# Batch 0's block attention in one pass per pair of heads, or in two passes over all heads

## The chip, the cores and the metric

One core of one Trainium2 chip runs the whole program. The metric is the device time in microseconds (us) of one execution, as the median of several runs. Engines: PE (TensorE), DVE (VectorE), ACT (ScalarE), POOL (GpSimd) and SP (SyncE, which here issues every load and store).

## What is computed

```python
# q, k, v: (4, 8, 576, 64); blocks of 64 tokens, block-causal
scores = np.where(mask, scale * q @ k.T, -1e9)      # mask: block_i >= block_j
attn = exp(scores - max) / (sum + 1e-9);  x = attn @ v      # x: (4*576, 512)
x = (sigmoid(x @ w_gate) * (x @ w_val)) @ w_out             # 512 -> 1536 -> 512
x = leaky_relu(x @ w_in) @ w_out2                           # 512 -> 2048 -> 512
```

All in float32. The weights must keep nearly float32 precision, so each weight unit and each activation is split into a high and a low float32r part, and a product is made of three matmuls.

## The kernel before, in words

The program is a list of operations, each with an engine (or a choice of two), a cost, a due time and the tiles that it uses. `Plan.order` (L127) then puts them in a row: again and again it takes the operation that can start first by its costs, and among those that can start at that moment the one with the smallest due time. That row is what each engine executes, strictly in its order. A tile comes from a `Ring` (L44) of a fixed number of buffers, and the tiles of a ring are given out in the order in which the program asked for them:

```python
if t.index != new[t.ring] or (k >= 0 and t.ring.tiles[k].left):   # L141
    waiting.add(o)
    return
```

so an operation that needs tile n of a ring waits until tile n-1 has been taken by its own first operation. The PSUM banks are rings too: `sc` (2 banks), `pa` (1), `tp` (2) and `mm` (3, L246).

`attention(b, ...)` (L332) works on a batch's eight heads in four pairs. `pair(i)` (L416) loads q and k of two heads (`tqk`, a ring of 3 buffers) and v (`tv`, a ring of 2) and handles the 576 queries in tiles: `query_tiles([0, 1])` (queries 0 to 255, keys up to 128 or 256), `query_tiles([2])`, `query_tiles([3])`, and `last_queries` (the last 64 queries of both heads together, all 576 keys). Each tile goes the same way:

- `scores`, L351: PE, q by k, into `sc` (batch 0 also uses `pa` for every third).
- `softmax`: DVE adds the mask and takes the row's extreme (L374); ACT makes the exponentials and their sum (L389); DVE adds 1e-9 and inverts (L399, L402); ACT or POOL multiplies (L407, L409).
- `transposed`, L500 (L458 for the last queries): PE transposes into `tp`; DVE or ACT copies out (`copy`, L296 for ACT, L298 for DVE).
- L522 (L472 for the last queries): PE, probabilities by v. In batch 0, the attention that stands alone, these go into `mm` banks.
- `split`: DVE or ACT writes the high part of x, DVE the low part (L309).

Batch 0's attention comes first (due times from 5 to 45 us); the attention of batches 1 to 3 is mixed into the matmuls of the batch before. The MLP's matmuls are `half_unit` (L917): one unit is 128 output columns, in two halves, tokens 0 to 255 and 256 to 575, each 12 matmuls into one `mm` bank (L938). The first gate units run all their first halves before the second ones (`by_half`). Each weight unit is loaded raw (`raw`, a ring of 3) and converted by ACT (`mag` L627, `rnd` L624), DVE (L628, L631, L635, split L298 and L309) and POOL (L641), then stored to `wd` for the later batches. All four engines thus share their time between attention and conversion.

Of the kernel before, what the change touches and what calls it, by code (L numbers as in the profile page):

```python
# [18 lines left out]
P = 128  # L19
BLK = 64  # L20
NKT = 5
# [177 lines left out]
def block_attention_then_two_mlps(  # L199
# [14 lines left out]
    B, H, _, D, S = qk.shape  # L214
# [69 lines left out]
    def load(t, dst, src, size, due, reads=(), writes=(), queue="sp"):  # L284
        if queue == "sp":
            op("sp", max(0.6, size / 320e3), lambda: nc.sync.dma_start(out=dst(), in_=src), reads, writes, [t], due, 1.8)
        else:
            op("act", 0.6, lambda: nc.scalar.dma_start(out=dst(), in_=src), reads, writes, [t], due, 1.8 + size / 320e3)
# [43 lines left out]
    def attention(b, start, length, alone):  # L332

        weight = [0.7, 0.9, 1.0, 1.1, 0.8]
        total = H // 2 * sum(weight)
        banks = [0]

        def bank():  # L340
            banks[0] += 1
            return (b_pa if alone and banks[0] % 3 == 0 else b_sc).tile()

        def scores(products, tqk, t):

            def f():
                for ps, col, row, a, q0, nq, k0, nk in products:
                    half = slice(a * D, a * D + D)  # L350
                    nc.tensor.matmul(  # L351
                        ps[row:row + nq, col:col + nk], lhsT=tqk[half, 0, q0:q0 + nq], rhs=tqk[half, 1, k0:k0 + nk],
                        start=True, stop=True,
                    )

            cost = 0.1 + sum(0.1 + 0.82e-3 * x[7] for x in products)
            used = list(dict.fromkeys(x[0] for x in products))
            op("pe", cost, f, [(tqk, 0), (tqk, 1)], used, [tqk, *used], t, kind="h")
# [54 lines left out]
                op(("act", "pool"), (0.24 + n / 1200, 0.25 + n / 1200), f, [r], [p_tok], [r, both], t + 2.6, port=("pool",))  # L413
            return [x[:2] for x in done]

        def pair(i):  # L416
            t_p = start + 2 * length * i / H

            t_end = 0.0 if alone else t_p + 2 * length / H
            at = [t_p + 2 * length * sum(weight[:c]) / (H * sum(weight)) for c in range(NKT)]  # L420

            tqk, tv = r_qk.tile(), r_v.tile()
            for a in range(2):
                load(
                    tqk, lambda a=a: tqk[a * D:a * D + D], qk[b, 2 * i + a].rearrange("s d n -> d s n"),
                    D * 2 * S * 4, t_p - 9, (), [(tqk, a)],
                )
            for a in range(2):
                load(tv, lambda a=a: tv[:, a], v[b, 2 * i + a], P * NKT * D * 4, t_p - 6, (), [(tv, a)])
            pas = {}  # L430

            def split(n0, n1, parts, t, p, reads):
# [47 lines left out]
            def query_tiles(cs):  # L480
                t = at[cs[0]]
                ps = [bank(), bank()]
                cols = dict(zip(cs, (0, P)))
                scores([(ps[a], cols[c], 0, a, c * P, P, 0, (c + 1) * P) for c in cs for a in range(2)], tqk, t)
                done = softmax([[(ps[a], cols[c], (c + 1) * P)] for c in cs for a in range(2)], True, t)
                for c in cs:
                    transposed(c, done[2 * cs.index(c):][:2], at[c])
# [41 lines left out]
                op("pe", cost, f, [(tv, 0), (tv, 1), *toks], [(pa, c)], [pa, tv, both], max(t + 5.2, t_end), kind="h")  # L529
                split(c0 * P, (c + 1) * P, ("C" if c0 else "A") if alone else "AC", max(t + 5.2, t_end) + 0.8, pa, [(pa, c)])  # L530

            for cs in ([0, 1], [2], [3]):
                query_tiles(cs)
            last_queries(at[NKT - 1])

        for i in range(H // 2):
            pair(i)

# [459 lines left out]


    attention(0, 5.0, FIRST, True)
    held, sl = {}, []
    sums_x = None
# [18 lines left out]
    for n, (u, half) in enumerate(order):  # L1023
        if n in stages:
            b = stages.index(n)
            length = starts[b + 1] - starts[b]
            if b:
                sg.append(r_sg.tile())
            if b < 2:
                sl.append(r_sg.tile(F32R))  # L1030
            if b == 0:
                attention(1, starts[0] + 3, length - SPREAD, False)
            elif b == 1:
                attention(2, starts[1] + 3, length / 2 - 3, False)
                attention(3, starts[1] + length / 2, length / 2 - SPREAD, False)
# [78 lines left out]
```

## Time and profile before

| what | value |
|---|---|
| median of 3 runs | 1036.53 us (1035.37 to 1037.73) |
| the profiled execution's own time | 1035.02 us |
| its span, first to last instruction | 1033.2 us |
| PE busy | 1015.0 us (98%) |
| DVE, ACT, POOL busy | 714.7, 529.0, 170.6 us |
| moved by DMA | 200.03 MB |

Busy times are those of the span. An engine's instructions overlap by a little, so the time that one takes of its engine is the distance from its start to the next start, which is a little less than its own duration. The profile's times are from the start of the span; the 1.8 us between span and own time lie around it.

### The profile page before, as it was taken

What the parts mean: (1) busy time and instruction counts of PE and PEld (TensorE: products, weight loads), DVE (VectorE), ACT (ScalarE), POOL (GpSimd) and SP (SyncE); (2) the same over time, 40 slices, a digit from 0 to 9 for tenths busy, and PEclk for the clock granted to TensorE, in tenths of its full rate; (3) what the DMA queues carried; (4) which work ended last, traced back from release to release, by engine and by line L of the source; (5) the groups of instructions that cost most, each with busy time, mean ns of one, the idle gap of its engine ahead of it and who ended that gap; (6) DMA issues with size and microseconds to landing.
All of it is one profiled execution on the core that took longest, in us unless ns stands there. A gap on an engine that the chain in (4) does not pass through costs nothing.

```text
span 1033.2 us, 20192 instructions
## 1 busy us (share of the span) xinstructions
PE 1015.0 (98%) x7680; PEld 939.7 (91%) x7680; DVE 714.7 (69%) x1767; ACT 529.0 (51%) x1187; POOL 170.6 (17%) x182
## 2 busy tenths in 40 slices
PE   7899999999999999999999999999999999999998
PEld 4579898999989889888988989999999999999998
DVE  6999899999987756467556448760844887163652
ACT  7987777687747564555556534242220454331320
POOL 3321122312231412112222102110200010000000
PEclk9999999999999999999999999999999999999999
DMA  8776878679787966566665445453441435251422
GB/s 246 239 242 232 313 267 272 214 245 312 257 286 273 307 226 225 193 187 216 227 207 186 144 143 188 144 187 98 154 164 62 154 108 188 72 164 65 164 79 93
DMA packets 69985, 200.03 MB, mean 194 GB/s; under 512 B 6912, under 2 KB 16128, under 8 KB 69888
## 3 DMA queue, kind: packets, MB, share of 16 engines
q1 hardware_dynamic: 69888, 198.73, 57.5%
q8 instruction: 61, 1.00, 0.4%
q14 instruction: 36, 0.29, 0.1%
HBM read 137.36 MB, written 61.34 MB: 192 GB/s over the span
## 4 chain that ended last, share of the span: by engine, by line
PE 83%; DVE 9%; ACT 4%; DMA 2%; issue 2%; POOL 0%; SPq 0%; ACTq 0%; DVEq 0%; POOLq 0%
PE mm L938 51%; PE mm L841 6%; PE tp L841 6%; PE sc L841 6%; PE sc L351 4%; PE pa L841 3%; PE tp L500 3%; PE pa L522 2%; DVE w L309 1%; DVE mag L635 1%; DVE both L374 1%; ACT both L389 1%; DVE mag L628 1%; ACT both L407 1%; PE tp L472 1%
## 5 line engine op out<-in xcount | busy, mean ns | idle before, releaser
L938 PE MATMUL mm<-x,w 128*128 128x256 f32 (+1 forms) x1920 | 271.1, 298 | 0.5 <-ACT gf L978 0.5
L938 PE MATMUL mm<-g,w 128*128 128x256 f32 (+1 forms) x1776 | 270.8, 298 | 0.0
L938 PEld LDWEIGHTS mm<-x,w 128*128 128x128 f32 x1920 | 257.0, 188 | 12.5 <-issue 4.9
L938 PEld LDWEIGHTS mm<-g,w 128*128 128x128 f32 x1776 | 245.7, 189 | 8.8 <-issue 2.0
L991 DVE TENSOR_TENSOR acc<-mm,acc 128x256 f32<-128x256 f32 (+1 forms) x160 | 72.6, 454 | 86.5 <-PE mm L938 85.8
L389 ACT ACTIVATE both<-both,nm 128x128 f32<-128x128 f32 (+2 forms) x144 | 83.0, 578 | 37.0 <-DVE nm L374 36.9
L641 POOL TENSOR_TENSOR wf<-mag,rnd 128x512 int32<-128x512 int32 x43 | 59.0, 1372 | 174.1 <-DVE mag L635 109.7
L841 PE MATMUL sc<-x,w 128*128 128x256 f32 (+1 forms) x480 | 76.3, 295 | 1.0 <-ACT v L296 1.0
L351 PE MATMUL sc<-qk 64*64 64x288 f32 (+4 forms) x356 | 69.3, 468 | 5.6 <-DMA qk<-in_qk 5.5
L309 DVE TENSOR_TENSOR g<-gf,g 128x576 fp32r<-128x576 f32 (+2 forms) x92 | 62.5, 685 | 17.3 <-ACT g L296 17.2
L374 DVE CUSTOM_DVE_ANT_0 both<-sc,mask 128x256 f32<-128x256 f32 (+3 forms) x133 | 59.1, 478 | 17.3 <-PE sc L351 17.3
L938 PE MATMUL mm<-sg,w 128*128 128x320 f32 (+1 forms) x416 | 70.2, 294 | 0.0
L841 PEld LDWEIGHTS sc<-x,w 128*128 128x128 f32 x480 | 67.8, 188 | 1.2 <-ACT v L296 1.2
L938 PE MATMUL mm<-qk,w 128*128 128x320 f32 (+1 forms) x384 | 66.8, 296 | 0.0
L296 ACT ACTIVATE g<-gf 128x576 fp32r<-128x576 f32 (+2 forms) x73 | 43.3, 596 | 45.2 <-DVE gf L965 23.0
L938 PEld LDWEIGHTS mm<-sg,w 128*128 128x128 f32 x416 | 60.5, 188 | 0.0
L409 POOL TENSOR_SCALAR both<-both,r 128x256 f32<-128x256 f32 (+4 forms) x54 | 36.8, 687 | 137.2 <-DVE r L402 101.0
L407 ACT ACTIVATE both<-both,r 128x512 f32<-128x512 f32 (+4 forms) x90 | 48.3, 575 | 17.3 <-DVE r L402 16.9
L938 PEld LDWEIGHTS mm<-qk,w 128*128 128x128 f32 x384 | 56.5, 189 | 0.0
L500 PE MATMUL tp<-ident,both 128*128 128x128 f32 x320 | 48.1, 280 | 5.0 <-ACT both L407 2.3
L627 ACT ACTIVATE mag<-raw 128x512 f32<-128x512 f32 x68 | 45.5, 669 | 12.3 <-DMA raw<-in_w 11.8
L309 DVE TENSOR_TENSOR w<-wf,w 128x512 fp32r<-128x512 f32 x68 | 49.0, 721 | 2.2 <-ACT w L296 1.9
(169 smaller groups left out, 1595.2 us busy)
## 6 DMA issues: line engine op xcount, KB each, us to landing
w<-wd SPq DMA_DIRECT2D x116, 512.0 KB, 4.2
raw<-in_w SPq DMA_DIRECT2D x68, 512.0 KB, 4.6
wd<-w SPq DMA_DIRECT2D x68, 512.0 KB, 4.2
ds<-raw SPq DMA_DIRECT2D x40, 512.0 KB, 4.8
w<-ds SPq DMA_DIRECT2D x40, 512.0 KB, 6.2
qk<-in_qk SPq DMA_DIRECT2D x32, 288.0 KB, 5.4
v<-in_v SPq DMA_DIRECT2D x32, 160.0 KB, 3.4
w<-wd SPq DMA_DIRECT2D x20, 256.0 KB, 3.6
```

What stands on the lines that cost most here:

```text
L296: nc.scalar.activation(dst(), src(), AF.Copy)
L309: engines[e].tensor_tensor(dst(), a(), f32(b()), ALU.subtract)
L351: nc.tensor.matmul(ps[row:row + nq, col:col + nk], lhsT=tqk[half, 0, q0:q0 + nq], rhs=tqk[half, 1, k0:k0 + nk], start=True, stop=True,)
L374: nc.vector.tensor_tensor_reduce(out=pt[:, n:n + width], in0=ps[:, col:col + width], in1=mask[:, 4 * P - width:] if masked else mask[:, :w ...
L389: nc.scalar.activation(pt[:, :n], pt[:, :n], AF.Exp, bias=nm[:, k - 1:k], scale=-1.0, accum_out=sm[:, i:i + 1],)
L407: nc.scalar.activation(pt[:, :n], pt[:, :n], AF.Copy, scale=r[:, i:i + 1])
L500: nc.tensor.transpose(tp[:, (j * m + k) * P:(j * m + k + 1) * P], tiles[a][0][:, j * P:(j + 1) * P], ident)
L627: op("act", c_act(n), lambda: nc.scalar.activation(mag[:], words(1).bitcast(F32), AF.Abs), [raw], [mag], [raw, mag], d - 8)
L641: engines[e].tensor_tensor(wf[:].bitcast(I32), mag[:].bitcast(I32), rnd[:], ALU.add)
L841: nc.tensor.matmul(p[:, :n], lhsT=wt[:, wl, col + k * P:col + (k + 1) * P], rhs=srcs[k][0]()[:, xl, hs], start=k == 0 and wl + xl == 0, st ...
L938: nc.tensor.matmul(ps[:, :n], lhsT=ws[:, wl, k * P:(k + 1) * P], rhs=srcs[k]()[:, xl, hs], start=k == 0 and wl + xl == 0, stop=k == 3 and ...
L991: op("dve", c_dve(n), lambda: nc.vector.tensor_tensor(a, ps[:, :n], a, ALU.add), [ps], toks_a, [ps], e)
```

## The change

`pair` takes a second argument, the query tiles that it handles. For batch 0 (`alone`) the four pairs are run through twice: first tiles 0 and 1 (queries 0 to 255) of all pairs, then tiles 2, 3 and the last queries. For the other batches there is still one pass. Each call of `pair` loads its own q, k and v: the first pass the first 256 tokens of them, the second all 576 tokens again. The due times are spread over the two passes in proportion to the tiles' weights.

```diff
-        def pair(i):
-            t_p = start + 2 * length * i / H
-
-            t_end = 0.0 if alone else t_p + 2 * length / H
-            at = [t_p + 2 * length * sum(weight[:c]) / (H * sum(weight)) for c in range(NKT)]
+        def pair(i, cs):
+            n, j = (S, NKT) if NKT - 2 in cs else ((cs[-1] + 1) * P, cs[-1] + 1)
+            share = sum(weight[cs[0]:j])
+            step = length * share / total
+            t_p = start + (length * (H // 2) * sum(weight[:cs[0]]) / total) + i * step
+
+            t_end = 0.0 if alone else t_p + step
+            at = [t_p + step * sum(weight[cs[0]:c]) / share for c in range(NKT)]
...
-                    tqk, lambda a=a: tqk[a * D:a * D + D], qk[b, 2 * i + a].rearrange("s d n -> d s n"),
-                    D * 2 * S * 4, t_p - 9, (), [(tqk, a)],
+                    tqk, lambda a=a: tqk[a * D:a * D + D, :, :n], qk[b, 2 * i + a].rearrange("s d n -> d s n")[:, :, :n],
+                    D * 2 * n * 4, t_p - 9, (), [(tqk, a)],
...
-                load(tv, lambda a=a: tv[:, a], v[b, 2 * i + a], P * NKT * D * 4, t_p - 6, (), [(tv, a)])
+                load(tv, lambda a=a: tv[:, a, :j], v[b, 2 * i + a][:, :j], P * j * D * 4, t_p - 6, (), [(tv, a)])
...
-            for cs in ([0, 1], [2], [3]):
-                query_tiles(cs)
-            last_queries(at[NKT - 1])
-
-        for i in range(H // 2):
-            pair(i)
+            for some in ([0, 1], [2], [3]):
+                if some[0] in cs:
+                    query_tiles(some)
+            if j == NKT:
+                last_queries(at[NKT - 1])
+
+        for cs in ([[0, 1], [2, 3]] if alone else [[0, 1, 2, 3]]):
+            for i in range(H // 2):
+                pair(i, cs)
```

Because the planner orders everything, a few lines move instructions on all engines. On PE, around the first gate matmuls, the row before reads (L351 scores, L500 and L458 transposes, L522 and L472 the products with v, L938 the MLP; the `sc<-qk` scores in it belong to batch 1):

```order
L351 MATMUL sc<-qk 128x128 x2
L351 MATMUL sc<-qk 128x256 x2
L522 MATMUL mm<-both,v 64x256 x6
L522 MATMUL mm<-both,v 64x128 x2
L458 MATMUL tp<-ident,both 128x128 x4
L458 MATMUL tp<-ident,both 64x128
L351 MATMUL sc<-qk 128x384 x2
L472 MATMUL mm<-last,v 64x64 x10
L938 MATMUL mm<-x_113,w 128x256 x48
```

and with the change (its lines are numbered 1 to 9 higher):

```order
L528 MATMUL mm<-both,v 64x256 x6
L528 MATMUL mm<-both,v 64x128 x2
L464 MATMUL tp<-ident,both 128x128 x4
L464 MATMUL tp<-ident,both 64x128
L352 MATMUL sc<-qk 128x512 x2
L478 MATMUL mm<-last,v 64x64 x10
L947 MATMUL mm<-x_113,w 128x256 x48
```

The first gate matmuls still stand right behind the last product of batch 0's last pair, with 48 matmuls of 256 columns, and batch 1 is one score step (128x512) further when they begin.

On ACT, the end of what stands ahead of those gate matmuls, before (L296 `last` is the copy that the last product needs):

```order
L407 ACTIVATE both<-both,r 128x576
L627 ACTIVATE mag<-raw 128x512
L389 ACTIVATE both,sm<-both,nm 128x128 x2
L389 ACTIVATE both,sm<-both,nm 128x256 x2
L296 ACTIVATE last<-tp 128x512
```

and with the change:

```order
L636 ACTIVATE mag<-raw 128x512
L633 ACTIVATE rnd<-raw 128x512
L390 ACTIVATE both,sm<-both,nm 128x384
L408 ACTIVATE both<-both,r 128x128
L296 ACTIVATE x_113<-mm 128x256
L408 ACTIVATE both<-both,r 128x256
L296 ACTIVATE last<-tp 128x512
```

Conversion steps and softmax steps of batch 1 now stand ahead of that copy, among them one exponential of 384 columns.

On SP, the first issues with the change:

```order
L286 DMA qk<-in_qk 64x2x256 x2
L286 DMA raw<-in_w 128x1024
L286 DMA v<-in_v 128x128 x2
L286 DMA qk<-in_qk 64x2x256 x2
L286 DMA v<-in_v 128x128 x2
L286 DMA raw<-in_w 128x1024
L286 DMA qk<-in_qk 64x2x256 x4
```

Before, the first was `qk<-in_qk 64x2x576 x2`, and the v behind the first `raw` was `128x320 x2`: the same first steps, with smaller transfers.

## Rows read from the trace of the kernel before

**Rows 1.** Windows: stretch, length; busy of PE, PEld, DVE, ACT, POOL; clock, DMA share, GB/s

```profile
26.00:52.00 26.00, 23.08 (x181) 13.64 (x181) 24.28 (x90) 24.58 (x67) 10.00 (x13) 0.93 0.77 242
52.00:64.00 12.00, 10.01 (x93) 6.80 (x91) 11.93 (x42) 10.93 (x29) 4.10 (x5) 1.00 0.76 243
...
104.00:130.00 26.00, 25.22 (x203) 22.45 (x202) 22.42 (x59) 21.23 (x43) 4.20 (x5) 1.00 0.90 311
...
182.00:260.00 78.00, 77.37 (x591) 71.90 (x587) 76.26 (x179) 59.17 (x135) 19.99 (x14) 1.00 0.76 259
260.00:312.00 52.00, 51.18 (x389) 46.90 (x388) 46.30 (x95) 30.62 (x62) 15.27 (x12) 1.00 0.77 265
```

**Rows 2.** Chain of waits, 0 to 72 us: start, length, what it ran through

```profile
1.55 4.71 DMA qk<-in_qk
...
13.89 0.60 ACT both L296
...
31.21 1.52 PE tp L500 x8
...
36.63 0.42 DVE x L298
...
62.27 0.48 ACT last L296
...
63.75 5.87 PE mm L938 x48
```

**Rows 3.** Who waited for whom on ACT, 0 to 64 us: total, times, longest

```profile
ACT both L407 <- DVE r L402: 1.9, 4, 0.7
```

**Rows 4.** ACT's timeline: start, length, instruction [idle before, releaser]

```profile
7.40 0.67 ACT L627 ACTIVATE mag<-raw 128x512 f32<-128x512 f32 x1 [5.17 <-DMA raw<-in_w]
...
15.09 0.60 ACT L407 ACTIVATE both<-both,r 128x384 f32<-128x384 f32 x1
15.59 0.67 ACT L627 ACTIVATE mag<-raw 128x512 f32<-128x512 f32 x1
16.17 0.65 ACT L624 ACTIVATE rnd<-raw 128x512 int32<-128x512 uint32 x1
...
22.33 1.20 ACT L407 ACTIVATE both<-both,r 128x128 f32<-128x128 f32 x3
23.42 0.62 ACT L389 ACTIVATE both<-both,nm 128x384 f32<-128x384 f32 x1
```

**Rows 5.** DMA issues of 0 to 64 us: count, KB each, median us to landing

```profile
qk<-in_qk SPq DMA_DIRECT2D x14, 288.0 KB, 6.0
...
v<-in_v SPq DMA_DIRECT2D x11, 160.0 KB, 2.9
```

**Rows 6.** DVE's timeline, near the end of batch 0's attention

```profile
60.56 0.41 DVE L631 TENSOR_SCALAR mag<-mag 128x512 int32<-128x512 int32 x1
60.90 0.41 DVE L298 CAST x<-mm 128x256 fp32r<-128x256 f32 x1
61.24 0.68 DVE L635 SCALAR_TENSOR_TENSOR mag<-raw,mag 128x512 int32<-128x512 int32 x1
...
63.50 0.56 DVE L374 CUSTOM_DVE_ANT_0 both<-sc,mask 128x384 f32<-128x384 f32 x1
```

**Rows 7.** PE's timeline

```profile
15.49 0.87 PE L522 MATMUL mm<-both,v 128*64 128x256 f32 x8
...
17.15 0.88 PE L500 MATMUL tp<-ident,both 128*128 128x128 f32 x6
18.59 1.06 PE L500 MATMUL tp<-ident,both 128*128 128x128 f32 x8 [0.57 <-DVE r L399]
...
23.52 1.13 PE L351 MATMUL sc<-qk 64*128 64x512 f32 x4
...
57.76 0.93 PE L351 MATMUL sc<-qk 64*128 64x128 f32 x8
```

**Rows 8.** Windows of PE alone: stretch, length; busy; clock, DMA share, GB/s

```profile
33.00:35.00 2.00, 2.00 (x8) 0.50 0.96 365
```

## The prediction

> **What bounds the kernel now.** I read the windows first, to find where the time can still move at all. Behind 64 us PE is busy almost without a break: it loses 0.8 us between 104 and 130, 0.6 between 182 and 260, 0.8 between 260 and 312 [rows 1], together 2.2 us. What is left is the opening stretch, 0 to 64 us, batch 0's attention, in which PE waits and no MLP matmul runs. The change touches only this stretch.
>
> There the windows show two engines at their limit, neither of them PE: between 26 and 64 us DVE is busy 36.2 of 38 us and ACT 35.5, while PE is busy 33.1, part of it at a lower clock [rows 1]. ACT's idle time in these 38 us is thus 2.5 us.
>
> The chain of waits says the same in order of time [rows 2]: it starts on the first q and k transfer, lies on PE until 13.9, on ACT from there to 31.2, on PE until 36.6, then on DVE, and at the end on ACT, whose copy of the last queries' probabilities (62.27 + 0.48) lets the last product and then the first gate matmuls go at 63.75. I call that moment the opening. The time of the whole kernel is the opening plus the PE work still to do then, plus what PE loses later. Of ACT's waits only those for DVE's inverted sums are worth naming, 1.9 us [rows 3]: an engine that waits this little shortens nothing by being reordered; only less work ahead of the opening, or an earlier start, would.
>
> **The change, part by part.**
>
> *Could the MLP start earlier?* This is what two passes could give: the first 256 tokens of x, all heads, are there long before the rest, and the 48 first gate matmuls of 5.9 us [rows 2] need only these. The instruction order says no. They stand behind the last product of the last pair, as before. The reason is in the words on the rings: gate units and batch 0's products share the `mm` ring, tiles are given out in the order asked for, and the attention asked first. PE's gaps ahead of the opening stay unused. So this term is 0, and the rest is a question of how much each engine has to do ahead of the opening.
>
> *Start.* The first two qk transfers shrink from 288 to 128 KB each, so 0.33 MB less lies ahead of the second of them and of the first raw weights, on which ACT's first real instruction waits until 7.40 [rows 4]. The second qk transfer took 4.71 us from issue [rows 2]. At some 300 GB/s (the windows show 242 to 311) 0.33 MB are 1.1 us. Bounds: 0, if the landing is all latency; 1.8, if 128 KB landed as the 160 KB of v do, in 2.9 us [rows 5]. I take -1.1, since at the start nothing else is in flight and bytes decide.
>
> *ACT ahead of the opening.* Counting ACT's instructions up to the copy of `last` (row 90 before, row 98 with the change): one exponential of 384 columns more (0.6), three more scalings of 128 columns (from 22.33 to 23.42 three took 1.1), one of 384 (0.50) and one of 576 (0.7, an estimate by length from that 0.50), one `mag` (0.58) and two `rnd` (0.55 each), two copies of 64 columns of x (0.1 each, an estimate); the copies out of `tp` change in shape, not in sum [rows 4]. That is +4.8 us, rounded with the overlap of the instructions to +4.7. None of it is new work: it is conversion for later units, softmax of batch 1, and scalings, which the planner shares out between ACT and POOL. But it now stands ahead of the copy that opens the MLP, on an engine that had 2.5 us to spare.
>
> *DVE ahead of the opening.* Up to its last copy of `last` (row 191 before, row 200 with the change): four more first steps of conversion (0.34 each), one third step (0.60), two reductions of 384 columns (0.48 each without the overlap), one pair of small operations on the sums (0.2), less two casts of 64 columns (0.3) [rows 6]. Together +2.8 us. DVE and ACT work side by side, so the two terms do not add; the larger one counts, ACT's.
>
> *Idle time.* ACT's 2.5 us could be squeezed to nothing, or the first pass, with its short tiles, could add as much again: bounds -2.5 and +2.5. I take 0: the row with the longest total is a wait on DVE [rows 3], and DVE gets more to do as well.
>
> *PE behind the opening.* The 512-column scores of batch 1 are done before it: -1.1 us [rows 7]. Everything else of PE's work is the same; the same matmuls, transposes and products are issued.
>
> *Later.* What ACT and DVE did early they need not do later, where DVE is busy 76.3 of 78 us [rows 1]. At most PE's 2.2 us of loss can come back, at least nothing. I take -0.3, since PE's losses there are many small ones.
>
> *DMA.* 16 transfers more, 8 of 128 KB and 8 of 64 KB, 1.6 MB, some 5 us of the stream's time in the first 30 us. SP issues them in order; the last q and k of the second pass waits for a free buffer until the first pair of that pass has all its scores. Behind it stand v of the second pass, a store and a raw load. The raw loads ahead of it cover six conversions, so I price this at 0; if the cover were gone, conversion would stop for about one landing of qk, 6 us [rows 5], at the worst.
>
> **Sum**, against the profiled execution's own 1035.0: -1.1 + 4.7 + 0 - 1.1 - 0.3 = +2.2, so 1037.2. The median of the runs shown is 1.5 above the profiled execution, so the predicted median is **1038.7 us**. With every term at its good end the sum is -1.8 + 4.7 - 2.5 - 1.1 - 2.2 = -2.9, at its bad end 0 + 4.7 + 2.5 - 1.1 = +6.1.
>
> **The rivals.**
>
> *PE's clock in the first pass (slower still).* At 31.2 us the chain passes from ACT to PE, which had been waiting, and PE then ran at half clock (0.50 in the window from 33 to 35 [rows 8], that is 1.2 GHz): eight transposes took 1.52 us [rows 2] where they take 1.06 at full clock [rows 7]. By that ratio the 5.4 us from 31.2 to 36.6 would have been 3.8: one such event cost 1.6 us. In the first pass PE has per pair 0.93 of scores, 0.88 of transposes and 0.87 of products [rows 7], 2.7 us, where ACT's share with one conversion is about 4.5 us (estimates by length [rows 4]: four exponentials 1.8, scalings and copies 1.6, `mag` and `rnd` 1.1). PE is thus idle two fifths of the time, more than now, and one or two more falls of the clock would add 1.6 to 3.2: +3.8 to +5.4, some 1041.3. Against it: at half clock the 2.7 become 5.4, and PE is busy again.
> The Trainium skill (TensorE: Matmul & The Clock Gate, "HAM oscillation — how this bites in real kernels") says that matmuls in bursts with waits between them fall back to the low clock again and again and pay for it each time. [...]
>
> *DVE stays the bound.* From 36.6 to 59 the chain lies on DVE. If ACT's extra work falls into its waits for DVE, DVE's +2.8 counts instead: -1.1 + 2.8 - 1.1 - 0.3 = +0.3, 1036.8. For it speaks the chain; against it that ACT has only 2.5 us of idle time for 4.7 us of work.
>
> *The early work pays (faster).* If ACT ran without a wait up to the opening and the conversions done early removed all of PE's later losses, the sum is -1.1 + 4.7 - 2.5 - 1.1 - 2.2 = -2.2, 1034.3. This decides for faster when ACT's idle time ahead of the opening falls to zero and PE's losses between 104 and 312 us vanish together. For it speaks that DVE is at its limit in that stretch; against it that PE loses so little there.
>
> **How the numbers follow.** About 0.2% (2.1 us) is what a measurement of this kernel can tell from no change, so faster is below 1034.5 and slower above 1038.6. Forecast case 0.58, half of it on either side of the slower bound, because its centre lies on it; clock 0.17, slower; DVE 0.13, no change; early work 0.12, nearly all faster. That gives faster 0.12, same 0.42, slower 0.46. Range 1034.3 to 1042.2: down to the faster rival, up to the clock rival's +5.4 with some idle time; beyond it on either side I leave a tenth.
>
> **What would show it.** Right: the first 48 gate matmuls still directly behind the last product of batch 0, starting between 65 and 68 us, with ACT busy over 95% up to there; the first reduction on DVE about 1 us earlier than 7.7; 512-column scores of batch 1 ahead of the opening; PE as good as unbroken behind it. Wrong: gate matmuls mixed into the second pass; an opening at or before 63.7; PE's clock at half for most of the first pass; ACT waiting for DMA between 20 and 50 us.

## The result and the profile after

The changed kernel is slower: 1043.86 us median (1042.49 to 1045.44, 4 runs) against 1035.95 for the kernel before on the same chip, a ratio of 1.0081 with a 95% interval of 1.0067 to 1.0096. The prediction was 1038.7 with a range up to 1042.2: the side was right, the size too small, and the result lies beyond the range.

| what | before | after |
|---|---|---|
| profiled execution, own time | 1035.02 | 1044.31 |
| its span | 1033.2 | 1042.3 |
| first gate matmul starts | 63.68 | 68.37 |
| from there to the end ("the rest" below) | 969.6 | 973.9 |
| PE's gaps ahead of (without its wait for the first q and k) / behind that matmul | 6.2 / 3.7 | 8.2 / 7.4 |
| DVE, ACT, POOL busy | 714.7, 529.0, 170.6 | 718.9, 525.0, 155.9 |

So the loss has two halves: 4.7 us at the opening, 4.3 behind it. In the second half 1.1 us more is hidden, as the 512-column scores of batch 1, which lay behind the opening, are now ahead of it.

The opening first. PE's timeline of the changed kernel (start, length, instruction, and in brackets the idle time before it with its releaser):

```profile
66.15 1.13 PE L352 MATMUL sc<-qk 64*128 64x512 f32 x4
67.49 0.95 PE L478 MATMUL mm<-last,v 128*64 128x64 f32 x20 [0.21 <-ACT last L296]
68.37 5.95 PE L947 MATMUL mm<-x,w 128*128 128x256 f32 x48
...
74.29 0.98 PE L947 MATMUL mm<-x,w 128*128 128x320 f32 x5
```

The gate matmuls still stand directly behind the last product, as in [rows 2]. The start gained little. ACT's and DVE's first instructions:

```profile
7.14 0.66 ACT L636 ACTIVATE mag<-raw 128x512 f32<-128x512 f32 x1 [4.91 <-DMA raw<-in_w]
...
6.23 0.29 DVE L375 CUSTOM_DVE_ANT_0 both<-sc,mask 128x128 f32<-128x128 f32 x1 [5.36 <-PE sc L352]
```

DVE starts 1.45 us earlier (7.68 before), ACT only 0.26 (7.40, [rows 4]): the raw weights land hardly sooner. DVE and POOL, further on, show something that the kernel before has only once up to there, at 62.4 us behind DVE's last copy of `last` (0.99 us):

```profile
40.18 1.15 DVE L400 TENSOR_SCALAR r<-sm 128x2 f32<-128x2 f32 x1 [0.23 <-ACT both L390]
...
45.87 1.24 DVE L400 TENSOR_SCALAR r<-sm 128x2 f32<-128x2 f32 x1 [0.20 <-ACT both L390]
```

```profile
40.03 1.26 POOL L650 TENSOR_TENSOR wf<-mag,rnd 128x512 int32<-128x512 int32 x1 [0.62 <-DVE mag L644]
45.80 1.28 POOL L650 TENSOR_TENSOR wf<-mag,rnd 128x512 int32<-128x512 int32 x1 [4.51 <-DVE mag L644]
```

An addition to two numbers per row, which takes 0.15 us elsewhere, lasts 1.15 and 1.24, and ends when POOL's long addition ends (40.03 + 1.26 = 41.29, 40.18 + 1.15 = 41.33). The Trainium skill (SBUF — State Buffer, "SBUF: two separate sides") says that DVE and GpSimd share one pair of ports, and that for the DVE instructions that use it whoever starts first holds the pair for the whole instruction while the other waits. These rows agree.

Behind the opening, the windows of the changed kernel (stretch, length; busy PE, PEld, DVE, ACT, POOL; granted clock, DMA share, GB/s):

```profile
26.00:52.00 26.00, 23.27 (x163) 12.34 (x163) 25.32 (x80) 23.74 (x57) 6.82 (x8) 1.00 1.01 301
52.00:68.00 16.00, 14.05 (x131) 9.06 (x130) 15.62 (x54) 15.68 (x44) 8.57 (x8) 1.00 0.91 279
...
104.00:130.00 26.00, 26.00 (x213) 24.25 (x212) 24.40 (x46) 18.19 (x35) 5.79 (x4) 1.00 0.87 295
130.00:182.00 52.00, 50.47 (x369) 46.70 (x368) 49.56 (x118) 41.13 (x84) 11.60 (x9) 1.00 0.78 266
182.00:260.00 78.00, 77.01 (x595) 70.34 (x593) 75.55 (x192) 58.48 (x134) 9.19 (x7) 1.00 0.79 268
260.00:312.00 52.00, 51.63 (x394) 47.56 (x393) 44.79 (x102) 28.94 (x59) 10.05 (x8) 1.00 0.74 250
312.00:400.00 88.00, 85.54 (x643) 75.23 (x643) 63.21 (x154) 54.02 (x122) 19.10 (x22) 1.00 0.73 248
```

Two stretches, neither of them in [rows 1], differ most: from 130 to 182 us PE loses 1.5 of 52 us, in the kernel before nothing, and from 312 to 400 us 2.5 of 88 us, in the kernel before 0.3:

```profile
130.00:182.00 52.00, 52.00 (x397) 47.98 (x395) 49.24 (x113) 39.22 (x77) 12.63 (x10) 1.00 0.79 270
...
312.00:400.00 88.00, 87.73 (x672) 78.06 (x671) 60.22 (x157) 55.81 (x124) 20.46 (x22) 1.00 0.78 267
```

The later one is the joint of two batches: batch 0's MLP ends (the kernel before stores its output from 331 to 345 us), batch 1's begins, and the sums of weight units are made for the later batches. PE's waits in the changed kernel from 305 to 402 us (who waited for whom, total, times, longest):

```profile
PE mm L947 <- ACT sg L956: 1.4, 1, 1.4
PE tp L506 <- ACT both L408: 0.8, 1, 0.8
PE tp L464 <- POOL both L410: 0.3, 1, 0.3
```

ACT and POOL, which PE waits for here, execute in order, so the instruction that PE needs can stand behind others. Which half of the loss comes from the two passes, and which from the new row of instructions that the planner makes for them, the trace does not tell; the experiments bear on that.

### The profile page after: what moved, and what is told of

Read it like the earlier page. It is cut to its first block, busy times and chain, and to the rows that moved or that the text cites. A ratio compares the mean times of both kernels' runs of the same rounds, so it can differ in the third digit from the quotient of the medians.

```text
span 1042.3 us, 20245 instructions
## 1 busy us (share of the span) xinstructions
PE 1019.6 (98%) x7680; PEld 940.8 (90%) x7680; DVE 718.9 (69%) x1781; ACT 525.0 (50%) x1184; POOL 155.9 (15%) x171
## 4 chain that ended last, share of the span: by engine, by line
PE 68%; DVE 4%; DMA 3%; ACT 2%; POOL 1%; issue 1%; SPq 0%; POOLq 0%; ACTq 0%; DVEq 0%
PE mm L947 39%; PE mm L850 6%; PE tp L850 6%; PE sc L850 6%; PE pa L850 3%; PE sc L352 3%; PE tp L506 2%; DMA w<-wd 2%; PE pa L528 2%; DMA raw<-in_w 1%; PE tp L478 1%; ACT both L390 1%; DVE w L309 1%; PE tp L464 0%; DMA ds<-raw 0%
## 5 line engine op out<-in xcount | busy, mean ns | idle before, releaser
L390 ACT ACTIVATE both<-both,nm 128x128 f32<-128x128 f32 (+4 forms) x144 | 83.0, 578 | 42.2 <-DVE nm L375 42.1
L650 POOL TENSOR_TENSOR wf<-mag,rnd 128x512 int32<-128x512 int32 x34 | 46.9, 1380 | 201.8 <-DVE mag L644 143.9
L375 DVE CUSTOM_DVE_ANT_0 both<-sc,mask 128x128 f32<-128x128 f32 (+3 forms) x132 | 58.4, 475 | 15.0 <-PE sc L352 14.7
L296 ACT ACTIVATE g<-gf 128x576 fp32r<-128x576 f32 (+2 forms) x69 | 40.2, 587 | 40.1 <-DVE gf L974 17.9
L408 ACT ACTIVATE both<-both,r 128x384 f32<-128x384 f32 (+4 forms) x91 | 49.6, 578 | 17.3 <-DVE r L403 17.2
L506 PEld LDWEIGHTS tp<-ident,both 128*128 128x128 f32 x320 | 37.1, 143 | 17.4 <-ACT both L408 6.8
```

What stands on the lines that cost most here:

```text
L296: nc.scalar.activation(dst(), src(), AF.Copy)
L375: nc.vector.tensor_tensor_reduce(out=pt[:, n:n + width], in0=ps[:, col:col + width], in1=mask[:, 4 * P - width:] if masked else mask[:, :w ...
L390: nc.scalar.activation(pt[:, :n], pt[:, :n], AF.Exp, bias=nm[:, k - 1:k], scale=-1.0, accum_out=sm[:, i:i + 1],)
L408: nc.scalar.activation(pt[:, :n], pt[:, :n], AF.Copy, scale=r[:, i:i + 1])
L506: nc.tensor.transpose(tp[:, (j * m + k) * P:(j * m + k + 1) * P], tiles[a][0][:, j * P:(j + 1) * P], ident)
L650: engines[e].tensor_tensor(wf[:].bitcast(I32), mag[:].bitcast(I32), rnd[:], ALU.add)
```

## The experiments

"First gate" is the start of the first gate matmul, "rest" the span less that, "gaps" the sum of PE's gaps behind it, all three from the one profiled execution; median and ratio are over the runs, against runs of the kernel before on the same chip. The rows are from several chips, on which the kernel before took 1034.7 to 1036.0, so kernels are compared by the ratio.

| kernel | median | ratio (95%) | first gate | rest | gaps |
|---|---|---|---|---|---|
| changed | 1043.86 | 1.0081 (1.0067 to 1.0096) | 68.37 | 973.9 | 7.4 |
| two_old | 1041.49 | 1.0060 (1.0042 to 1.0078) | 68.83 | 970.9 | 4.9 |
| one_new | 1042.63 | 1.0072 (1.0051 to 1.0093) | 63.92 | 977.4 | 9.2 |
| before_f42 | 1035.57 | 1.0003 (0.9993 to 1.0014) | 64.08 | 968.6 | 3.4 |
| after_f42 | 1043.84 | 1.0085 (1.0067 to 1.0103) | 68.94 | 972.5 | 6.6 |
| gates_free | 1043.84 | 1.0084 (1.0069 to 1.0099) | 31.68 | | |
| gates_free2 | 1039.72 | 1.0049 (1.0032 to 1.0065) | 29.74 | | |
| after_s54 | 1043.78 | 1.0083 (1.0068 to 1.0098) | 68.89 | 974.2 | 7.9 |
| after_rport | 1044.68 | 1.0090 (1.0075 to 1.0105) | 65.70 | 976.1 | 7.1 |
| two_strict | 1041.19 | 1.0055 (1.0038 to 1.0072) | 69.79 | 972.9 | 6.0 |
| two_strict_rport | 1039.28 | 1.0043 (1.0028 to 1.0058) | 66.46 | 972.0 | 5.5 |
| before_rport | 1044.02 | 1.0085 (1.0067 to 1.0103) | 65.18 | 976.9 | 9.2 |
| before_s54 | 1034.98 | 1.0003 (0.9994 to 1.0013) | 64.42 | 970.1 | 4.1 |
| before_rport_wlat | 1035.56 | 1.0011 (1.0001 to 1.0020) | 64.41 | 969.0 | 3.9 |
| after_wlat | 1040.12 | 1.0055 (1.0040 to 1.0070) | 68.77 | 970.5 | 5.4 |
| before_wlat | 1033.05 | 0.9982 (0.9971 to 0.9993) | 64.21 | 967.4 | 2.5 |
| after_rport_wlat | 1038.89 | 1.0036 (1.0022 to 1.0050) | 68.32 | 968.1 | 3.1 |
| gates_rport_wlat | 1037.95 | 1.0026 (1.0017 to 1.0036) | 29.43 | | |
| before_wlat_again | 1032.87 | 0.9974 (0.9965 to 0.9983) | 64.12 | 967.5 | 2.7 |

**Passes or row?** The planner's result was split at the first gate matmul, and each half combined with the other kernel's: two passes with the rest in the one-pass kernel's order, and one pass with the rest in the two-pass kernel's. `tail` is that order, written out.

```diff
-        for o, e in plan.order():
+        for o, e in plan.order(count, EARLY, TAIL):
...
-        return result
+        return result + [(self.ops[count + i], e) for i, e in tail]
```

> Two passes for batch 0, but what stands ahead of its end on every engine besides batch 0's own attention is the one-pass kernel's set, and everything behind it stands in the one-pass kernel's exact order, on the same engines. Theory O (order): the 7.9 us come from the newly planned row, 4 us of ACT work of later steps put ahead of the first gate matmul and an unlucky order behind it, not from the two passes. Then the first gate matmul starts at 63.5 to 65 us (one pass 63.75, two passes 68.37), from there to the end it takes 969 to 970.5 us, and the time is that of one pass within 2 us. Theory P (passes): short tiles, double loads and PE waiting in the first pass cost it. Then the first gate matmul starts at 67 us or later, and the time is 3 us or more above one pass, although the rest of the row is the old one.

> The mirror image: batch 0 in one pass, with the two-pass kernel's set of other work ahead of its end (18 operations more) and the two-pass kernel's exact order behind it. Theory O: the first gate matmul starts at 66 to 68 us, from there to the end 973 to 974.5 us, time 6 to 9 us above one pass, about that of two passes. Theory P: first gate matmul at 64 us, and a time within 5 us of one pass, more only by what the order behind it costs (up to 5).

Each half of the loss went, in the main, with its own half of the kernel. With two passes and the old rest, the opening stays late (68.83) and the rest is nearly the old one (970.9); with one pass and the new rest, the opening is where it was (63.92) and the rest costs 7.8 us more. Of these, 2.7 lie directly behind the opening, where the 512-column scores and other work that the two-pass kernel does ahead of it stand among the gate matmuls: from the first gate matmul to the first of 320 columns it takes 8.64 us (72.56 less 63.92), in the other three kernels 5.92. From that second point to the end it takes 968.0 in the changed kernel and 968.7 here with the new row, 963.6 in the kernel before and 965.0 in two_old with the old one. So neither theory alone: the passes make the late opening, and most of the loss behind it comes with the new row. The old row is not free of it either: two_strict and two_strict_rport, below, have the one-pass kernel's order behind the opening and a rest of 972.9 and 972.0.

**Is the new row's loss chance?** One constant of the planner, the spread of batch 0's due times, from 40 to 42 in both kernels:

```diff
-FIRST = 40.0
+FIRST = 42.0
```

> One pass, with batch 0's due times spread over 42 instead of 40 us: no work is added or taken, the planner only lays out another row. If the order behind the first gate matmul is a matter of chance, the stretch from there to the end differs from 969.4 by 1 to 5 us in either direction, with the first gate matmul within 1.5 us of 63.75. If the two-pass kernel's loss there has a cause of its own, the stretch stays within 1 us of 969.4.

> Two passes, with batch 0's due times spread over 42 instead of 40 us. By chance of the order: the stretch behind the first gate matmul differs from 973.9 by 1 to 5 us, and is as likely to be shorter. With a cause of its own in the two passes: it stays above 973. The first gate matmul within 1.5 us of 68.4 either way.

Nothing moved by more than 1.5 us, in either kernel; nor did it when the MLP's due times were shifted:

```diff
-STARTUP = 50.0
+STARTUP = 54.0
```

> The changed kernel with the time at which the planner lets the MLP's due times begin moved from 50 to 54 us. Theory D (behind the opening PE loses time because the due times no longer fit an opening that is later by 4.7 us): the rest, first gate matmul to end, falls from 973.9 to 970.5 us or less, and the time to about 1040. Theory C (the order that the planner falls into behind the opening differs by chance with each edit): the rest lies anywhere from 968 to 977, and PE's longest waits stand at other places than in the changed kernel.

> The kernel before (one pass), with the time at which the planner lets the MLP's due times begin moved from 50 to 54 us. Theory T: first gate matmul at 63.5 to 66 us and a rest between 968 and 977, most of any loss at the joint of two batches (310 to 360 us). Theory U: a rest within 1.5 us of 969.6.

That the due times no longer fit a later opening is thus out: the rest stayed at 974.2 and 970.1. It is not chance in the sense that any edit of the planner draws it anew; that some do is shown below.

**Was the ring what kept the gate units from starting early?** In the second pass the products take other PSUM banks than the gate units; the second kernel keeps the scores out of `pa` there as well and puts the products into it.

```diff
-                px = (b_mm if alone else b_tp).tile()
+                px = b_tp.tile()
...
-                    pas[0] = (b_mm if alone else b_pa).tile()
+                    pas[0] = (b_mm if alone and j < NKT else b_tp if alone else b_pa).tile()
```

> Two passes as in the change, but the second pass takes its product banks from the transposes' ring, so that the first-half gate units no longer queue behind batch 0's products in the mm ring and stand mixed into the second pass. Theory R (the ring is what keeps the two passes from paying): the first gate matmul starts at 35 to 45 us, the 48 first-half gates (5.9 us) fill PE's waits ahead of the opening, and the time is 1037 to 1040. Theory B (DVE and ACT bound the second pass, and gates there only delay the transposes and scores that they wait for, or end as later idle time of PE): the gates start early all the same, but the last product of batch 0 comes 3 us or more later than with the change, and the time is 1042 to 1045.

> As the run before it, with the products of the second pass in pa and tp banks by kind, and its scores in sc banks only. Theory R: 1037 to 1040, with the last product of batch 0 within 3 us of that of the change. Theory B: 1042 to 1046. A difference between the two kernels of over 2 us would say that the banks that the products take, and not the early gates, set the time.

The ring was the obstacle: the first gate matmuls start at 31.7 and 29.7, mixed into the second pass. But it hardly pays. In the second kernel the last product and the first gate matmuls of the second half stand at

```profile
71.49 0.95 PE L479 MATMUL tp<-last,v 128*64 128x64 f32 x20
72.37 0.44 PE L507 MATMUL tp<-ident,both 128*128 128x128 f32 x2
72.74 1.13 PE L352 MATMUL sc<-qk 64*128 64x512 f32 x4
73.80 6.43 PE L948 MATMUL mm<-x,w 128*128 128x320 f32 x42
```

73.80, against 74.29 in the changed kernel, where 5.95 us of gate matmuls come after the opening, and about 69.6 in the kernel before (63.68 + 5.9). PE is not the engine that the second pass waits for, so what it does early shortens little; in the first of the two kernels this point even comes at 75.99. In the profiled executions the second kernel's span is 4.9 us shorter than that of the changed kernel; 0.5 of these lie ahead of this point and the rest behind it, where its row is another one. The two kernels differ by 4.1 us in time, more than the 2 us named in the expectation of the second: which banks the products take counts for more than the early gates, as the first has those too and gains nothing. (A fall of the granted clock to 0.69 from 63 to 68 us in the first kernel's profiled execution has a part in its 75.99.)

**Did the extra work ahead of the opening make it late?** This was the prediction's main term. Here the planner may place ahead of the first gate matmul, besides batch 0's attention, only the 116 operations of conversion and of batch 1 that stood there in the one-pass kernel; behind it comes the one-pass kernel's order.

```diff
+        allowed = [o for o in self.ops if o.index < count - 2 or o.index - count in early]
...
-        for _ in self.ops:
+        for _ in allowed:
```

> Two passes, with ahead of the first gate matmul exactly the 116 other operations (conversion, batch 1) that stood there in the one-pass kernel, and behind it the one-pass kernel's order. Theory W (the opening is late because conversion and batch 1 work was drawn ahead of it, as forecast): first gate matmul at 62.5 to 65 us, ACT busy ahead of it about 53 us, time 1035 to 1037. Theory P (two passes themselves cost it, by their waits): first gate matmul at 67 to 69.5 us, ACT idle ahead of the opening 5 us or more, time 1039 to 1042.

Windows of this kernel, and of the kernel before, from ACT's start to its last copy of `last`:

```profile
7.00:69.30 62.30, 55.37 (x369) 31.78 (x370) 55.39 (x196) 55.46 (x153) 20.08 (x24) 0.97 0.88 260
```

```profile
7.00:62.75 55.75, 50.32 (x361) 29.45 (x358) 52.17 (x193) 52.74 (x144) 20.92 (x24) 0.97 0.83 252
```

With the same work ahead of it the opening was as late as ever (69.79): ACT and DVE are each busy for 3 us longer, and idle for 3 to 4 us more. This execution is the slowest of its kernel's four (1044.67), with a granted clock of 0.66 from 63 to 68 us, so a part of the 69.79 may be the clock's; two_old, with nearly the same work ahead and a full clock there, opens at 68.83, and by its median two_strict is still 0.55% over the kernel before. The work that was drawn ahead is thus not what holds the opening; the two passes are.

**Do the stalls on the shared port matter?** The planner keeps POOL's and DVE's long instructions apart if they are marked with `port`; the addition to the sums was not.

```diff
-            ), [(sm, i) for i in range(m)], [r], [r, sm], t + 2.2)
+            ), [(sm, i) for i in range(m)], [r], [r, sm], t + 2.2, port=True)
```

> The changed kernel with the addition and inversion of the sums on DVE marked as needing the port that DVE shares with POOL, so that the planner places none of POOL's long additions over them. Theory S (stalls of these small instructions on the shared port lengthen the passes): none of them lasts over 0.3 us, their sum ahead of the opening falls from 2.7 to about 0.8 us, and the first gate matmul starts at 66 to 67 us. Rival (the stalls lie in time that ACT would wait anyway, or the planner's other places for POOL's work cost as much): the opening stays at 68 to 69 us.

> The run before it, with the addition of 1e-9 to the sums marked as needing the port that DVE shares with POOL. If stalls on that port are the main part of what the two passes cost, none of the additions lasts over 0.3 us, the first gate matmul starts 1.5 to 3 us earlier than in the run before it, and the time falls by as much; if they lie in time that ACT and PE wait anyway, it falls by less than 0.7 us.

The eight additions to two numbers ahead of the opening last 3.5 us together in the changed kernel and in two_strict, and 1.4 and 1.6 with the mark; the first gate matmul falls to 65.70 and 66.46 (one addition to four numbers still lasts 0.98 in the changed kernel with the mark, so not all stalls are gone). In time, two_strict gains 1.9 us, within the intervals of the two; the changed kernel gains nothing, as its rest came out 2.2 us longer. And a single opening is not so sure: after_rport_wlat, below, has the same instructions up to there and opens at 68.32. PE's matmuls of the second are 1.2 us behind those of the first at 38 us, at full clock in both, and 2.6 at 44 us; between the two its granted clock falls (stretch, length; busy; clock, DMA share, GB/s):

```profile
38.00:43.00 5.00, 4.57 (x46) 1.00 1.05 385
```

```profile
38.00:43.00 5.00, 3.33 (x28) 0.69 1.04 384
```

That the fall alone makes a late opening is not shown: the kernel before has one [rows 8] and opens at 63.68, before_wlat, below, has the same instructions up to there and none, and opens at 64.21. So the stalls are shown; their price, 1 to 2 us, is not beyond the measurement.

**The same mark in the kernel before** was meant to show that it does nothing there.

> The kernel before (one pass), with the same mark on the addition to the sums. There these additions took 1.5 us together ahead of the first gate matmul, with none over 0.3 us, so the opening can gain nothing: first gate matmul at 63 to 64.5 us. Theory T (behind the opening the planner's order differs with every edit, and the kernel before holds a good one): the rest, 969.6 before, comes out between 968 and 977, time 1034 to 1042. Theory U (only two passes or an order made for them lose time behind the opening): rest within 1 us of 969.6, time 1034.5 to 1036.5.

It lost 9 us: one pass, opening at 65.18, later than expected, and a rest of 976.9. (The expectation overlooks the addition of 0.99 us at 62.4.) A one-pass kernel with one mark for the planner thus loses more behind the opening, 7.3 us, than the changed kernel does. DVE's timeline at the place, 351 to 356 us:

```profile
351.37 0.15 DVE L399 TENSOR_SCALAR r<-sm 128x1 f32<-128x1 f32 x1
355.19 0.69 DVE L675 TENSOR_TENSOR wf<-w 128x512 f32<-128x512 f32 x1 [3.67 <-DMA w<-wd]
355.80 0.16 DVE L402 RECIPROCAL r<-r 128x1 f32<-128x1 f32 x1
```

and ACT's and PE's:

```profile
356.05 0.78 ACT L407 ACTIVATE both<-both,r 128x576 f32<-128x576 f32 x1 [4.39 <-DVE r L402]
```

```profile
356.88 1.33 PE L458 MATMUL tp<-ident,both 128*128 128x128 f32 x5 [3.39 <-ACT both L407]
```

Read from the bottom: PE waits 3.39 us for ACT's scaling, ACT 4.39 for the inverted sum, and that stands on DVE behind the sum of a weight unit (L675) whose reload had not landed. DVE had been free since 351.52. In all, DVE's waits of that kind from 305 to 402 us were

```profile
DVE wf L675 <- DMA w<-wd: 9.7, 6, 3.7
```

The planner reckons with 1.64 us for the 512 KB, 1.8 more until they have landed and 0.18 between instructions, 3.6 in all. In the changed kernel, from 300 to 400 us, the median was 4.2 from issue (count, KB each, median us):

```profile
w<-wd SPq DMA_DIRECT2D x19, 512.0 KB, 4.2
```

so by its costs such a sum is ready when it is not, and it puts it in front of an instruction that would have been.

**Repair of that alone.** The planner's 1.8 becomes 4.5 for reloads, 6.3 us in all; nothing of the work changes, and nothing ahead of the opening.

```diff
-            load(ws, lambda: f32(ws[:]), wd[k], P * 8 * n, d - 16, [("wd", k)], [(ws, 0), (ws, 1)])
+            load(ws, lambda: f32(ws[:]), wd[k], P * 8 * n, d - 16, [("wd", k)], [(ws, 0), (ws, 1)], lat=4.5)
```

> The one-pass kernel with the mark on the sums (rest 976.9 us behind the opening, 1044.0), and in addition the planner reckons with 4.5 instead of 1.8 us until a reloaded weight unit has landed. Only the order behind the opening can change. Theory L (PE loses its time at the joints of the batches because DVE stands at the sum of a reloaded weight, with the softmax's inversion queued behind it, and ACT and PE behind that): DVE's waits for reloaded weights between 305 and 402 us, of which the longest were 3.7 and 2.1, shrink to under 1 us each, PE's wait of 3.4 at 357 us is gone, the rest falls to 972 or less and the time to 1036 to 1040. Theory C (any new order draws a new loss somewhere): rest 968 to 978, with waits of that kind at other places or PE waiting for other things.

> The changed kernel, with the planner reckoning with 4.5 us until a reloaded weight unit has landed. First gate matmul unchanged at 68 to 69 us. Theory L: the rest falls from 973.9 to 969 to 971 (the 512-column scores being done ahead, 968.5 would be the kernel before's), time 1039 to 1041. Theory C: rest 968 to 977.

> The kernel before, with the planner reckoning with 4.5 us until a reloaded weight unit has landed. Theory L: as PE loses 3.7 us in all behind its opening, of it 0.3 between 312 and 400 us, it gains nothing: 1034 to 1036.5. Theory C: a rest between 968 and 977, 1034 to 1042.

At the same place the one-pass kernel with the mark now reads (DVE, then PE)

```profile
347.57 0.15 DVE L399 TENSOR_SCALAR r<-sm 128x1 f32<-128x1 f32 x1 [0.94 <-ACT both L389]
347.64 0.68 DVE L298 CAST x<-pa 128x512 fp32r<-128x512 f32 x1
348.24 0.15 DVE L402 RECIPROCAL r<-r 128x1 f32<-128x1 f32 x1
```

```profile
348.31 1.69 PE L938 MATMUL mm<-x,w 128*128 128x256 f32 x12
349.84 0.71 PE L458 MATMUL tp<-ident,both 128*128 128x128 f32 x5
```

The inversion follows its addition by 0.7 us instead of 4.4, PE doesn't wait, and from 305 to 402 us DVE waits for no reload at all. The rest falls from 976.9 to 969.0, the ratio from 1.0085 to 1.0011. The changed kernel's rest falls by 3.4 us (ratio 1.0081 to 1.0055, with intervals that just touch). The kernel before, for which no gain was expected, gains about 2 us. DVE's waits for reloads over the whole run, in the kernel before and in the changed kernel, were

```profile
DVE wf L675 <- DMA w<-wd: 17.2, 12, 3.5
DVE wf L684 <- DMA w<-wd: 24.8, 16, 3.3
```

and with the longer latency 0.6 and 1.6. In the stretch from 305 to 402 us the two kernels differed little (6.3 and 6.9), and PE lost 0.8 there in the kernel before. So these waits are in both kernels, and how much of them reaches PE depends on what stands behind them. In more rounds:

> The one-pass kernel with 4.5 us until a reloaded weight unit has landed, once more and in more rounds: 1032 to 1034, a ratio to the kernel before of 0.997 to 0.9995, rest 967 to 968.5 us.

1032.87 us, a ratio of 0.9974 (0.9965 to 0.9983): the one-pass kernel with the planner's longer latency is faster than both kernels.

**Both repairs, and the two passes at their best.**

> The changed kernel with both planner edits: the mark on the sums (alone it brought the first gate matmul from 68.4 to 65.7 us and nothing in time), and 4.5 us until a reloaded weight unit has landed (alone 3.7 us less). If the loss of the change is these two things and little else, first gate matmul at 65 to 67 us, rest at 969.5 us or less, time 1036 to 1038, so that 1 to 3 us over the kernel before remain for the two passes. If they are not independent, the time stays at 1039 to 1041.

> The two passes at their best: early gate units (as in the second kernel with free gates, 1039.7), and both planner edits. If the early gates pay once nothing else is late, the first 320-column gate matmuls start before 71 us and the time is 1033 to 1036, under the kernel before. If DVE and ACT set the pace of the second pass whatever PE does meanwhile, the last product of batch 0 comes at 70 to 72.5 us, and the time is 1036.5 to 1040.

The two repairs add up only in part (1038.89; its first gate matmul and its time lie above what was expected, its rest is as expected), and 3.3 us (2.6 by the ratios) remain over the one-pass kernel with the same two edits (1035.56). With early gate units on top it is 1037.95; DVE in its second pass, and the start of the second half's gate matmuls:

```profile
26.00:52.00 26.00, 22.42 (x185) 16.25 (x187) 25.97 (x78) 23.24 (x53) 8.79 (x8) 1.00 1.04 331
```

```profile
73.43 6.87 PE L948 MATMUL mm<-x,w 128*128 128x320 f32 x45
```

DVE is busy 25.97 of 26 us. The early gates fill gaps of PE in a stretch that DVE and ACT set.

**The same edit in both kernels.** Set side by side, the table gives what the two passes cost under each planner edit (one pass, then two):

| edit in both | opening | rest | ratio |
|---|---|---|---|
| none | 63.68, 68.37 | 969.6, 973.9 | 1, 1.0081 |
| 42 for 40 | 64.08, 68.94 | 968.6, 972.5 | 1.0003, 1.0085 |
| 54 for 50 | 64.42, 68.89 | 970.1, 974.2 | 1.0003, 1.0083 |
| longer latency | 64.21, 68.77 | 967.4, 970.5 | 0.9982, 1.0055 |
| mark | 65.18, 65.70 | 976.9, 976.1 | 1.0085, 1.0090 |
| both repairs | 64.41, 68.32 | 969.0, 968.1 | 1.0011, 1.0036 |

With the longer latency in both, 3.1 of the 4.3 us behind the opening remain: the reloads account for about 1.2 us of that difference, not for most of it. With the mark in both, or both repairs, the rest of the two passes is the shorter one, by 0.8 and 0.9 us. The loss behind the opening thus goes with the row that the planner happens to make, not with the two passes as such; the late opening stays in all pairs but the one with the mark alone.

## Why the prediction was wrong in size

- **What bounds the opening**: right. DVE and ACT at their limit, PE not; gates_rport_wlat shows it from the other side.
- **Could the MLP start earlier: 0**: right, and for the reason given, the `mm` ring; freeing it moved the gates by 37 to 39 us, and the time not at all in one kernel and by 3.3 us (by the ratios) in the other, for which the early gates are not shown to be the reason.
- **Start, -1.1**: ACT gained 0.26. Of the two bounds the latency one was nearer.
- **ACT ahead of the opening, +4.7**: the net of this and the start was to be 3.6, and 4.7 was measured, so the size looks good. The cause falls, so that the size is luck: with the extra work taken away (two_strict) the opening stayed late. What the two passes cost there is stalls of DVE's small additions behind POOL (2 us in the rows, 1 to 2 in time at most) and some 3 us that remain with both repairs. Of those a part may be work that the planner hands to ACT, which is busy for 3 us longer with the same operations ahead, and a part the clock in some executions; how much each is stays open.
- **PE's clock as a rival**: its number, 1041.3, was nearest, by luck, as its mechanism was not seen: the granted clock is 1.00 from 26 to 68 us in the changed kernel, while the kernel before has a fall there [rows 1, 8]. Falls do occur, in one execution and not in another of the same instructions (0.69 and 1.00 above). The price of 1.6 us for one is of the right size at its place: before_wlat, without it, is 1.3 us later than the kernel before at 29 us and level with it at 36. But it is partly won back, and the openings differ by 0.5.
- **PE behind the opening, -1.1, and Later, -0.3**: this is the step that failed. The scores did move ahead of the opening, but the text gave Later bounds of 0 to -2.2 ("At most PE's 2.2 us of loss can come back, at least nothing"), and the rest grew by 4.3 us, where -1.4 was forecast. That is 5.7 of the 7.1 us by which the forecast fell short (+2.2 against +9.3 in the profiled executions); 1.1 lie at the opening. It took the row of instructions behind the opening as given, though the planner makes the whole row anew, and a new row can lose more as well as less. (The 2.2 itself is from windows that leave out what lies behind 312 us; in all, PE's gaps behind the opening were 3.7.) With the rows exchanged, the loss went with the row in the main (two_old, one_new). What in the row makes it is shown in part: in four pairs of kernels that differ in the latency of reloads alone the rest falls by 2.2 us (kernel before), 3.4 (changed kernel), 7.9 (before_rport) and 8.0 (after_rport), so each row holds DVE at reloads that have not landed. But the one-pass kernel gains by it too, and of the difference of 4.3 it explains about 1.2. The changed kernel's longest waits of PE, 1.4 us at 326 and 1.0 at 135, stand on ACT behind conversion steps and exponentials and not behind a reload; with the longer latency the first is gone and the second is not. What sets these off stays open.

## What to carry to other kernels

Where a planner or scheduler writes the instruction order, the term for "everything behind the change" has no bound of zero: compare its rows there too, above all at joints, and price the waits of in-order engines that stand in front of others' work. A planner's latency that is too short for loads shows as an engine idle on a DMA with ready work queued behind it; make it no shorter than the trace has it, and judge an edit with the same planner settings on both sides, and with more than one setting: here the two passes cost between 0.05% and 0.8%. And before splitting a stage to let the next one start early, see whether the engine that sets the stage is the one that gets the gaps.

## What the runs showed that had not been expected

- A mark on one small instruction, with all work the same, cost the one-pass kernel 9 us (1044.02 against 1034.93), and with one latency constant changed it is back at 1035.56.
- An addition of 0.15 us lasts up to 1.24 us while POOL's 1.28 us addition runs.
- Kernels with the same instructions up to the opening opened at 65.70 and 68.32 us; one profile's opening is good to about 2.5 us. (The opening of the two passes without the mark, 68.37 to 69.79 in six profiled executions, is later than that of one pass, 63.68 to 65.18 in eight, by more.)
